# Whole GpSimd additions, ordered by semaphores against VectorE's two-input passes, in an attention and MLP kernel

## The chip, the cores and the metric

The kernel runs on one core of one Trainium2 chip. The metric is device microseconds for one execution. Lower is better. The kernel before takes 679.54 us (median of three runs, 679.36 to 679.79).

A core has five instruction queues that are used here. TensorE (PE in the profile; its weight loads are PEld) multiplies matrices into PSUM, eight banks of 128 x 512 f32. [...] SyncE (SP) issues the DMAs. Each queue runs its instructions in order, and queues wait for one another through semaphores.

## The reference

x is 2048 rows of 640 in bf16. It is normalised once, and attention with 32 heads of width 20, all sharing one key and one value head, and an MLP with squared relu run side by side on it:

```python
xn = _layernorm(x)                              # 2048 x 640
q = (xn @ wq).reshape(B, S, 32, 20).transpose(0, 2, 1, 3)
k, v = xn @ wk, xn @ wv                         # 2048 x 20 each
p = softmax(einsum("bhqd,bkd->bhqk", q, k) * 20 ** -0.5)
attn = einsum("bhqk,bkd->bhqd", p, v) ... @ wo  # 640 x 640
h = relu(xn @ w1 + b1) ** 2                     # 2048 x 1536
out = x + attn + (h @ w2 + b2)
```

The largest part by far is the exponential: 32 heads x 2048 x 2048 scores.

## The kernel before, in words

**The work.** The queries are cut into 4 chunks of 512, the heads into 8 groups of 4. That gives 32 blocks b (chunk b // 8, group b % 8). A block has 16 tiles, each of 128 keys for its four heads. One head of one tile, a "head tile" of 128 keys x 512 queries, is one matmul of kT with qT into one PSUM bank (line 1318, written QK below). Two to four such matmuls of different heads are issued at once, side by side in rows of the array; this is a batch. There are 2048 head tiles in all.

**Two ways to the exponential.** Most tiles go the ACT way: ScalarE reads two or three neighbouring PSUM banks and writes exp to the ring PT of RING slots (line 1595). Then one group of four column-tiled matmuls (one for each head) multiplies the tile by the values (line 1896, PT,vx, written PV below). The other tiles, D tiles, go the VectorE way. For each of their four heads VectorE converts the scaled scores to int16, so that the bits read as bf16 are a rough power of two (line 1694, function S_P1). This is the base pattern, 128 x 2048 int16, in one of NPB pattern buffers pbx. Three shifted copies are made by adding 32, 64 and 96 to every int16, and the four patterns, each with its own weight, are summed by PV: one group with vx, three with vp. So a D tile needs four conversions on VectorE, three shifted passes, and four PV groups, where an ACT tile needs one PV group and ScalarE's time.

**The shifted passes.** A pass is made by VectorE (line 1715, functions S_PH and S_STEAL) or by GpSimd (line 1777, function S_PHP), which adds four int16 at a time as one int64. GpSimd's part is placed under VectorE instructions of lines that read PSUM: the function beneath looks how much of such an instruction is left and the function cut takes as many columns as fit; the rest follows in pieces.

**Port users.** The planner marks some VectorE instructions `port=True`: the shifted passes (1715), the squares of the MLP (1106, two inputs), the normalisation product of a block (1957 and 1986, two inputs) and the layernorm's scaling (743). A GpSimd piece waits for the latest of these; none of these waits for GpSimd by a semaphore, they are only planned after the piece.

**The order.** No order is written out by hand. A planner (class Sched) runs when the kernel is built. Streams (S_QK, S_EXP, S_P1, S_PH, S_PHP, S_PV, S_MISC and others) offer their next request with a duration; the planner takes, engine by engine, the one that can start first, and among those within 15 ns the one with the best priority. The resulting list of each engine is what the engine executes, with a semaphore wait for each dependence that isn't implied already. PLAN holds one row of settings for each half block, 64 rows; `seed` and `nz` in it replace some choices by pseudo-random others.

Settings that the change touches: `W32` (when VectorE's planned backlog is below this many ns, a QK batch gives ScalarE two banks rather than three, and bank 2 to a D head tile), `DPH` (share of D tiles with a pass on VectorE of its own), `PHQ` (with more waiting passes than this, or less than STL = 3000 ns left in the block, VectorE takes one), `NQS` (slots of qT, filled by DMA from qpk by the function spread), RING, NPB.

**Between and after.** The MLP, the query projection and the output projection are units, which S_MISC starts when the position among the blocks reaches their due time (line 962 holds their matmuls). For the last chunk six of the eight output half tiles (128 rows x 320 columns) are made in two parts: u_P1 ahead of the end (h @ w2, plus those attention tiles that are ready, plus the residual, kept in f32 in `part`), and u_PF behind the last block. The two others (NPX = 1, u_PX) are summed wholly in PSUM, the residual through the identity. The last three blocks are normalised by VectorE's transposes alone (norm_last), the others through small DMAs.

Of the kernel before, what the change touches and what calls it, by code (L numbers as in the profile page):

```python
# [52 lines left out]
RING = 25  # L53
NPB = 10
# [7 lines left out]
NQS = 6  # L62
# [9 lines left out]
PAT = 27.6  # L72
# [2115 lines left out]
```

## Time and profile before

| what | value |
|---|---|
| three runs | 679.36, 679.79, 679.54 us; median 679.54 us |
| profiled execution | 681.03 us; its span, first to last instruction, 679.3 us |
| granted TensorE clock | 0.997 |
| PE busy | 668.8 us, 98% |
| ACT busy | 659.5 us, 97% |
| DVE busy | 607.0 us, 89% |
| POOL busy | 452.2 us, 67% |
| DMA | 29.90 MB, 44 GB/s |

Read it so: busy time is the union of an engine's instructions over the span. Matmuls are pipelined, so a busy PE is not yet a PE at its peak; the start-to-start distances in a timeline tell more. A group is one line with one operation; a mean is that of one instruction. A wait names the engine and line that ended the idle time. A busy sum divided by the count is the pace of instructions that overlap at their ends, and is a little below the mean duration.

### The profile page before, as it was taken

The page shows a single profiled execution, that of the slowest core. Times are in us where ns is not written, and L with a number is a line of the kernel's source. Part 1 is how long each engine was busy: PE and PEld are TensorE (multiplying, and loading weights), DVE is VectorE, ACT ScalarE, POOL GpSimd, SP SyncE. Part 2 cuts the span into 40 slices and gives each one's busy share as a digit, 9 for nine tenths or more (in the row PEclk, how much of TensorE's full clock was granted, in tenths as well). Part 3 has the DMA queues.
Part 4 walks back from the last instruction along what each step waited for, and adds up shares of the span by engine and source line. Part 5 has one row for each costly group of instructions (what it writes and reads, how often), then busy time and mean ns, then how long its engine had stood idle before and what let it go on. Part 6 is the DMA issues. An engine that isn't in the chain of part 4 may idle for free.

```text
span 679.3 us, 23577 instructions
## 1 busy us (share of the span) xinstructions
PE 668.8 (98%) x9953; PEld 226.4 (33%) x9953; DVE 607.0 (89%) x1097; ACT 659.5 (97%) x664; POOL 452.2 (67%) x827
## 2 busy tenths in 40 slices
PE   8999999999999999999999999999999999999998
PEld 5322222233223333332223333333222333333434
DVE  7978999999999998989999888888999899997895
ACT  6989999999999999999999999999999999999995
POOL 2073775787577866777778886786666877687700
PEclk9989999999999999999999999999999999999999
DMA  7282244111110111111000112111110011111001
GB/s 222 51 145 76 56 113 102 29 22 28 30 21 16 43 42 23 47 42 26 20 20 18 28 46 46 26 34 42 30 25 18 20 39 37 32 42 47 12 2 41
DMA packets 39891, 29.90 MB, mean 44 GB/s; under 512 B 23562, under 2 KB 34795, under 8 KB 39787
## 3 DMA queue, kind: packets, MB, share of 16 engines
q1 hardware_dynamic: 39787, 28.39, 18.0%
q8 instruction: 80, 1.31, 0.8%
q14 instruction: 24, 0.20, 0.1%
HBM read 11.12 MB, written 2.62 MB: 20 GB/s over the span
## 4 chain that ended last, share of the span: by engine, by line
PE 64%; ACT 33%; DVE 2%; DMA 1%; issue 0%; POOL 0%; DVEq 0%
ACT PT L1595 32%; PE ps L1896 25%; PE ps L1318 20%; PE ps L962 19%; DMA xnT<-big 1%; DVE pbx L1694 1%; DMA pbx<-in_A_x_dram 0%; DVE stats L708 0%; PE ps L999 0%; DVE out_sb L1156 0%; PE ps L1813 0%; DVE OTs L1957 0%; DVE pbx L1715 0%; POOL pbx L1777 0%; DVE mv L711 0%
## 5 line engine op out<-in xcount | busy, mean ns | idle before, releaser
L1595 ACT ACTIVATE PT<-ps 128x1024 bf16<-128x1024 f32 (+1 forms) x642 | 653.0, 1189 | 7.1 <-PE ps L1318 6.7
L1777 POOL INT64_ADD pbx<-pbx x803 | 447.3, 576 | 171.4 <-DVE pbx L1715 74.9
L1694 DVE TENSOR_SCALAR pbx<-ps 128x512 int16<-128x512 f32 x619 | 407.0, 684 | 49.9 <-PE ps L1318 45.9
L1318 PE MATMUL ps<-qT,kT 20*128 20x512 bf16 x2048 | 250.0, 385 | 2.5 <-ACT PT L1595 2.2
L1896 PE MATMUL ps<-pbx,vp 128*32 128x512 bf16 x1860 | 169.7, 383 | 0.2
L1318 PEld LDWEIGHTS ps<-qT,kT 20*128 20x128 bf16 x2048 | 62.6, 91 | 242.4 <-ACT PT L1595 164.8
L1896 PE MATMUL ps<-PT,vx 128*32 128x512 bf16 x1428 | 136.2, 384 | 0.4 <-ACT PT L1595 0.3
L962 PE MATMUL ps<-w_sb,big 128*32 128x320 bf16 x1536 | 74.7, 302 | 0.0
L962 PE MATMUL ps<-xnT,w_sb 128*32 128x512 bf16 x960 | 73.7, 383 | 0.1
L1715 DVE TENSOR_SCALAR pbx<-pbx 128x2048 int16<-128x2048 int16 x98 | 66.5, 691 | 0.5
L1896 PEld LDWEIGHTS ps<-pbx,vp 128*32 128x32 bf16 x1860 | 45.5, 95 | 51.6 <-issue 30.6
L1896 PE MATMUL ps<-pbx,vx 128*32 128x512 bf16 x620 | 60.5, 385 | 0.1
L1896 PEld LDWEIGHTS ps<-PT,vx 128*32 128x32 bf16 x1428 | 36.1, 95 | 43.9 <-issue 31.4
L962 PEld LDWEIGHTS ps<-w_sb,big 128*32 128x32 bf16 x1536 | 32.7, 95 | 28.4 <-issue 22.0
L1098 DVE TENSOR_SCALAR hT_tmp<-ps,b1col 128x512 bf16<-128x512 f32 x48 | 35.6, 742 | 1.2 <-PE ps L962 0.9
L962 PE MATMUL ps<-wo_p,OTp 120*32 120x320 bf16 (+1 forms) x640 | 31.8, 301 | 0.1
L962 PE MATMUL ps<-xnT,wq_sb 128*32 128x512 bf16 x375 | 28.5, 383 | 0.0
L962 PEld LDWEIGHTS ps<-xnT,w_sb 128*32 128x32 bf16 x960 | 18.6, 95 | 27.3 <-issue 17.7
L1896 PEld LDWEIGHTS ps<-pbx,vx 128*32 128x32 bf16 x620 | 16.2, 95 | 18.7 <-issue 12.0
L1941 DVE COPY Tn<-ps 128x512 f32<-128x512 f32 x29 | 19.8, 682 | 0.5 <-PE ps L1896 0.5
L1106 DVE TENSOR_TENSOR big<-hT_tmp 128x512 bf16<-128x512 bf16 x48 | 20.2, 425 | 0.0
L962 PEld LDWEIGHTS ps<-wo_p,OTp 120*32 120x32 bf16 (+1 forms) x640 | 14.7, 95 | 11.6 <-issue 4.7
(95 smaller groups left out, 188.9 us busy)
## 6 DMA issues: line engine op xcount, KB each, us to landing
Rb<-kT SPq DMA_DIRECT2D x29, 256.0 KB
xres<-in_A_x_dram SPq DMA_DIRECT2D x16, 160.0 KB
out_dram<-out_sb SPq DMA_DIRECT2D x16, 160.0 KB
qT<-qpk SPq DMA_DIRECT2D x105, 20.0 KB
pbx<-in_A_x_dram SPq DMA_DIRECT2D x3, 640.0 KB
w_sb<-in_B_w_dram SPq DMA_DIRECT2D x1, 1920.0 KB
w_sb<-in_B_w_dram SPq DMA_DIRECT2D x4, 480.0 KB
OTp<-OTs SPq DMA_DIRECT2D x96, 20.0 KB
```

What stands on the lines that cost most here:

```text
L962: return lambda e: e.matmul(ps[32 * j:32 * j + m, b_[0], 0:n], Lj, R, start=first, stop=last, tile_position=(0, 32 * j))
L1098: v = yield Req(("dve", 658.0, 742.0, [lambda e: e.tensor_scalar(out=hT_tmp[:, k, :], in0=ps[:, b_[0], :], scalar1=b1col[:, f:f + 1], scal ...
L1106: w = yield Req(("dve", SQ_D, SQ_D + 82.0, [lambda e: e.tensor_tensor(out=h2T[:, qc % 2, f, :], in0=hT_tmp[:, k, :], in1=hT_tmp[:, k, :], ...
L1318: ins.append(lambda e, i=i, b=b, t=t, h=h: e.matmul(ps[:, i, :], kT[32 * h:32 * h + DH, t * 128:(t + 1) * 128], qT[32 * h:32 * h + DH, b % ...
L1595: op = yield Req(("act", d_, d_ + 107.0, [lambda e, slot=slot, n=n, src=src: e.activation(out=PT[:, slot:slot + n, :], in_=ps[:, src, :], ...
L1694: return Req(("dve", d_, d_ + 82.0, [lambda e: e.tensor_scalar(out=PB[:, k, hsl, :], in0=ps[:, bk:bk + np_, :], scalar1=OFFS, scalar2=0.0, ...
L1715: return Req(("dve", 600.0, 684.0, [lambda e: e.tensor_scalar(out=PB[:, k, :, :], in0=PB[:, s, :, :], scalar1=PH_D[j], scalar2=None, op0=A ...
L1777: return lambda e: e.int64_add(PB8[:, k, c0 // 4:c1 // 4], PB8[:, s, c0 // 4:c1 // 4], int(PH_D[j]) * 0x0001000100010001)
L1896: ins = [(lambda e, h=h, first=first, last=last: e.matmul(ps[32 * h:32 * h + 32, bk, :], lhs, rhs[h], start=first, stop=last, tile_positio ...
L1941: v = yield Req(("dve", 600.0, 682.0, [lambda e: e.tensor_copy(out=Tn[:, tb, :], in_=ps[:, pvb, :])]), (lambda: None if oldt() is None els ...
```

## The change

- GpSimd's pass is one instruction over all 2048 columns (`PUN = False`), and an ordinary request: it may start at any time, no longer only beneath another VectorE instruction.
- A GpSimd pass and VectorE's port users are chained: each waits, by a semaphore, for the latest one before it when that is on the other engine (`last_port`). So a port user on VectorE now waits for a GpSimd pass that is under way.
- DPH goes from 0.3 to 0 and PHQ from 4 to 8: VectorE makes a pass only in the last block, near the end of a block, or when more than eight are waiting.
- 11 pattern buffers for 10; to make room, RING goes from 25 to 23 and NQS from 6 to 4.
- W32 goes from 2000 (in 58 rows of 64) to 650 or 700 (in 63); `seed` is nonzero in 44 rows rather than 40, with new values, and a few rows have other settings of their own.
- NPX goes from 1 to 0: all eight half tiles of the last chunk go by u_P1 and u_PF, u_P1 is due at 26.5 rather than 27.6, and u_PF may begin before its u_P1 is done. Its matmuls have priorities of their own (PFA, PFB).
- PVK, PVR, PVS, PVG and PFE are new; the helper `where` keeps the position and its PLAN row, which were worked out anew at each call.

```diff
-RING = 25
-NPB = 10
+RING = 23
+NPB = 11
...
-NQS = 6
+NQS = 4
...
-PAT = 27.6
+PAT = 26.5
...
-    (640, 3500.0, 600.0, 6000.0, 0, 900.0, 12, 2, 0.0, 3, 60.0, 600, 4.0, 2000.0, 2, 0.3, 0, 0.0, 0.0, 4, 0.5, 2, (0, 3, 400.0, 300.0), 1, 0, 8, 1.0, 2.0, 2, 99, 2000.0, -1, 400.0, 600.0),
+    (640, 3500.0, 600.0, 6000.0, 0, 900.0, 12, 2, 0.0, 3, 60.0, 600, 4.0, 650.0, 2, 0.0, 0, 0.0, 0.0, 8, 0.5, 2, (0, 3, 400.0, 300.0), 1, 0, 8, 1.0, 2.0, 2, 99, 2000.0, -1, 400.0, 600.0),
...
-NPX = 1
+NPX = 0
+PUN = False
+PFA, PFB, PFE = 0.6, -1.0, 0
+PVK, PVR, PVS, PVG = 1, 16, 1, 0
...
+            if not PUN and self.last_port is not None and (eng == "pool" and rr.name == "PHP" or rr.port) and self.last_port.eng != eng:
+                deps = deps + [self.last_port]
...
-            if eng == "dve" and rr.port:
+            if rr.port or not PUN and rr.name == "PHP":
                 self.last_port = op
...
-            v = yield from groups(g_wo(qc, st, cs, ts), 320, b_, [], 2, f"PF_{st}_{hh}", gdeps=[(lambda t=t: get(*tiles_of(qc, t, st))) for t in ts])
+            v = yield from groups(g_wo(qc, st, cs, ts), 320, b_, [], 2, f"PF_{st}_{hh}", fp=[PFA + .01 * (st % 4)] * (len(ts) - 1) + [PFB + .01 * (st % 4)], gdeps=[(lambda t=t: get(*tiles_of(qc, t, st))) for t in ts])
+            yield Until(lambda: f"PP{st}_{hh}" in done)
...
+        def pvres():
+            return int(not pvbank and (sum(len(v) for v in pv_items.values()) >= PVK - PVS or sum(slot_busy) >= PVR - 4))
...
-                    nres = (plan("D67") if wanted[0] else 0) + (not pvbank)
+                    nres = (plan("D67") if wanted[0] else 0) + pvres()
...
-                    c1 = cut(2048, F_, E_)
+                    c1 = cut(2048, F_, E_) if PUN else 2048
...
-                    return Req(("pool", d_, d_ + 60.0, [part(0, c1, k, s, j)]), [acc[-1]] + pbres[k].last, 2 if left_ns(b) > PHU else -1, "PHP", under=True)
+                    return Req(("pool", d_, d_ + 60.0, [part(0, c1, k, s, j)]), [acc[-1]] + pbres[k].last, 2 if left_ns(b) > PHU else -1, "PHP", under=PUN)
...
+                        if i == 0 and 2 <= b < NBLK - 1 and len(pv_items[b]) < PVK and sum(slot_busy) < PVR:
+                            return None
...
-        for k in range(8 - 2 * NPX):
-            st, hh = 4 * q3 + NPX + k // 2, k % 2
+        for k in range(8 - NPX):
+            st, hh = 4 * q3 + (k + NPX) // 2, (k + NPX) % 2
...
-            yield Until(lambda: "QKend" in done and not expq and not units)
+            yield Until(lambda: "QKend" in done and not expq and (not PFE or not units))
...
-                yield Until(lambda: f"PP{st}_{hh}" in done)
+                yield Until(lambda: (st, hh) in ptiles if PFE == 0 else f"PP{st}_{hh}" in done)
```

More of the change, by code (lines that the diff above doesn't have):

```diff
@@ L966, in pe_n, with groups @@
             return PE512 if n > 400 else PE320 if n > 300 else 0.5 * PE512 + 5.0
-        def groups(gl, n, b_, deps, p, name, m=32, gdeps=None, nj=4):
+        def groups(gl, n, b_, deps, p, name, m=32, gdeps=None, nj=4, fp=None):
             v = None
@@ L972, in mk @@
                     return Req(("pe", pe_n(n), pe_n(n) + PELAT, col4(L, R, n, b_, k == 0, k == len(gl) - 1, m, nj)),
-                              dd, p if pos() < 0.5 or k == 0 and not late(b_) else min(p, pick("%s%d" % (name, k), plan("MISCP"), plan("MISCP"), 0.5, 1.05) if k else LATEP), name, mode="col", cols=512.0 if n > 400 else 320.0)
+                              dd, fp[k] if fp else p if pos() < 0.5 or k == 0 and not late(b_) else min(p, pick("%s%d" % (name, k), plan("MISCP"), plan("MISCP"), 0.5, 1.05) if k else LATEP), name, mode="col", cols=512.0 if n > 400 else 320.0)
                 gd = (lambda k=k: [] if gdeps is None else gdeps[k]() if callable(gdeps[k]) else gdeps[k])
@@ L1283, in past, with where @@
                 cur_a[0] += 1
+            where()
+        spot = [0.0, None]
+        def where():
+            if cur_a[0] == NSB:
+                spot[0] = float(NBLK)
+            else:
+                f = cur_a[1] / float(HPG * len(seqs[cur_a[0]]))
+                spot[0] = cur_a[0] + f if not SB else 2.0 * f if cur_a[0] == 0 else cur_a[0] + 1.0 + f
+            spot[1] = PLAN[min(NBLK * PSEG - 1, int(spot[0] * PSEG))]
         def pos():
-            if cur_a[0] == NSB:
-                return float(NBLK)
-            f = cur_a[1] / float(HPG * len(seqs[cur_a[0]]))
-            return cur_a[0] + f if not SB else 2.0 * f if cur_a[0] == 0 else cur_a[0] + 1.0 + f
+            return spot[0]
         def plan(name):
-            return PLAN[min(NBLK * PSEG - 1, int(pos() * PSEG))][name]
+            return spot[1][name]
+        where()
         def pick(key, *opts):
@@ L1437, in poll_l @@
                     dbk = sorted([x for x in MREG if x in fb], key=freeat)
-                    dbk = dbk[:max(0, len(dbk) - (not pvbank))]
+                    dbk = dbk[:max(0, len(dbk) - pvres())]
                     if not dbk or nd_ok < 1 or sum(len(v) for v in pv_items.values()) > plan("sq"):
@@ L2048, in due @@
                 return d >= 0
-            return d >= plan("mlate") or d >= -plan("mearly") and sum(len(v) for v in pv_items.values()) <= plan("mq")
+            return d >= plan("mlate") or d >= -plan("mearly") and sum(len(v) for k_, v in pv_items.items() if PVG == 0 or k_ in pvbank) <= plan("mq")
         def S_MISC(until=None):
@@ L2065, in ready @@
                             return True
-                        return any(due(units[j]) and have(*units[j][3]) for j in range(min(len(units), 16)))
+                        return any(due(u) and have(*u[3]) for u in units[:16])
                     yield Until(ready)
@@ L2104, in S_PX @@
             st, hh = 4 * q3 + k // 2, k % 2
-            yield Until(lambda: (pos() >= PXAT[k] and have(*[f"PP{st}_{hh}" for st in range(4 * q3 + NPX, ST) for hh in range(2)]) or "QKend" in done) and have(f"xr{st}") and have(*[f"H{q3}_{f}" for f in range(FT)]))
+            yield Until(lambda: (pos() >= PXAT[k] and have(*[f"PP{st}_{hh}" for st in range(4 * q3, ST) for hh in range(2) if 2 * (st % 4) + hh >= NPX]) or "QKend" in done) and have(f"xr{st}") and have(*[f"H{q3}_{f}" for f in range(FT)]))
             hb = Hold([None])
@@ L2110, in S_TAIL @@
         def S_TAIL():
-            for k in range(2 * NPX):
+            for k in range(NPX):
                 sc.spawn(S_PX(k), "PX")
-            yield Until(lambda: "QKend" in done and not expq and not units)
+            yield Until(lambda: "QKend" in done and not expq and (not PFE or not units))
             def g(st, hh):
-                yield Until(lambda: f"PP{st}_{hh}" in done)
+                yield Until(lambda: (st, hh) in ptiles if PFE == 0 else f"PP{st}_{hh}" in done)
                 yield from u_PF(st, hh, Hold([None]))
-            for st in range(4 * q3 + NPX, ST):
-                for hh in range(2):
-                    sc.spawn(g(st, hh), "PF")
+            for k in range(NPX, 8):
+                sc.spawn(g(4 * q3 + k // 2, k % 2), "PF")
             yield Until(lambda: all(f"out{st}" in done for st in range(ST)))
```

126 rows, old and new, of the table PLAN are left out of this document.

## The prediction

> **What bounds the kernel now.** I read the engine totals first, then one long stretch without the start and the end, then the chain.
>
> ```profile
> PE 668.8 (98%) x9953; PEld 226.4 (33%) x9953; DVE 607.0 (89%) x1097; ACT 659.5 (97%) x664; POOL 452.2 (67%) x827
> ...
> PE 64%; ACT 33%; DVE 2%; DMA 1%; issue 0%; POOL 0%; DVEq 0%
> ```
>
> ```profile
> 60.00:640.00 580.00, 578.69 (x8604) 187.59 (x8604) 529.85 (x901) 577.94 (x571) 424.85 (x759) 1.00 0.16 36
> ```
>
> In the stretch the columns are PE, PEld, DVE, ACT, POOL. ACT works 577.94 of 580 us and PE 578.69. POOL isn't on the chain and DVE has 2% of it, so nothing that only shortens GpSimd's or VectorE's work can show, unless it takes work from ACT and PE too. The groups say what that work is:
>
> ```profile
> L1595 ACT ACTIVATE PT<-ps 128x1024 bf16<-128x1024 f32 x498 | 482.0, 1096 | 5.3 <-PE ps L1318 5.0
> L1595 ACT ACTIVATE PT<-ps 128x1536 bf16<-128x1536 f32 x144 | 216.6, 1513 | 1.8 <-PE ps L1318 1.7
> ```
>
> ```profile
> L1595 ACT ACTIVATE PT<-ps 128x1024 bf16<-128x1024 f32 (+1 forms) x642 | 653.0, 1189 | 7.1 <-PE ps L1318 6.7
> L1777 POOL INT64_ADD pbx<-pbx x803 | 447.3, 576 | 171.4 <-DVE pbx L1715 74.9 <-DVE big L1106 30.2 <-DVE pbx L1694 23.7
> L1694 DVE TENSOR_SCALAR pbx<-ps 128x512 int16<-128x512 f32 x619 | 407.0, 684 | 49.9 <-PE ps L1318 45.9
> L1318 PE MATMUL ps<-qT,kT 20*128 20x512 bf16 x2048 | 250.0, 385 | 2.5 <-ACT PT L1595 2.2
> L1896 PE MATMUL ps<-pbx,vp 128*32 128x512 bf16 x1860 | 169.7, 383 | 0.2
> L1715 DVE TENSOR_SCALAR pbx<-pbx 128x2048 int16<-128x2048 int16 x98 | 66.5, 691 | 0.5
> L1106 DVE TENSOR_TENSOR big<-hT_tmp 128x512 bf16<-128x512 bf16 x48 | 20.2, 425 | 0.0
> L1957 DVE TENSOR_TENSOR OTs<-Tn,Rb 128x512 bf16<-128x512 f32 x23 | 16.2, 704 | 0.1
> L1813 PE MATMUL ps<-kT,zeros 128*32 128x512 bf16 x76 | 6.8, 385 | 0.0
> ```
>
> 498 x 2 + 144 x 3 = 1428 head tiles go through ACT in 642 instructions; 653.0 / 1428 = 0.457 us each, 1.83 us for a tile of four. The other 620 are 155 D tiles with 1860 / 4 = 465 shifted passes, 98 by DVE and 367 by POOL. ACT idles 679.3 - 653.0 = 26.3 us beside its exponentials, mostly at the start and the end. So time = 26.3 us + 0.457 us x the head tiles on ACT: to be faster, the schedule must make more D tiles.
>
> PE must agree to that:
>
> ```profile
> 655.29 0.40 PE L1896 MATMUL ps<-pbx,vp 128*32 128x512 bf16 x4
> ...
> 655.62 0.39 PE L1318 MATMUL ps<-qT,kT 20*128 20x512 bf16 x3
> ...
> 655.94 0.40 PE L1896 MATMUL ps<-PT,vx 128*32 128x512 bf16 x4
> ...
> 656.17 0.39 PE L1896 MATMUL ps<-pbx,vx 128*32 128x512 bf16 x4
> ...
> 656.38 0.39 PE L1896 MATMUL ps<-PT,vx 128*32 128x512 bf16 x4
> ```
>
> Start to start, a PV group takes 0.21 to 0.23 us, and a QK batch pushed between two costs 0.33 + 0.32 - 0.23 = 0.42 us, whether it holds two heads or four. There is about one batch for each exponential, 2048 / 642 = 3.19 heads in a batch. A D tile costs PE three more PV groups, 3 x 0.22 = 0.66 us. PE thus gains only when batches are fuller. What keeps them from being full:
>
> ```profile
> PEld ps L1318 <- ACT PT L1595: 164.8, 434, 0.9
> PEld ps L1318 <- DVE pbx L1694: 55.6, 142, 0.5
> DVE pbx L1694 <- PE ps L1318: 45.9, 104, 1.3
> ```
>
> 142 batches waited last for a conversion by DVE to free a bank, and DVE 104 times for a batch: the three engines are coupled. (These waits of PEld overlap matmuls still running, so they aren't lost PE time.) DVE's 98 shifted passes stand among the conversions and make them late.
>
> **The change, part by part.**
>
> *Passes taken off VectorE.* Those that stay are bounded below by the last block's, which the diff leaves on DVE:
>
> ```profile
> 640.00:679.30 39.30, 8.41 (x13) 0.99 0.06 19
> ```
>
> These are 13 instructions of line 1715; above, 44, if the end of each of the 31 other blocks makes one too. I take 20, near the row, because with PHQ at 8 a backlog of nearly three tiles is allowed. So 78 go, at 66.5 / 98 = 0.679 us each: DVE gains 53 us (37 to 58).
>
> *Passes on GpSimd.* 803 pieces now make 367 passes, 447.3 / 367 = 1.22 us a pass without the gaps between pieces.
>
> ```profile
> L1777 POOL INT64_ADD pbx<-pbx x803: 263/572/1048, 33.2 to 645.6; - x161
> ```
>
> The longest, 1048 ns, is a whole pass. 445 passes at 1.05 us are 467 us, 20 more than now, in the 612 us between 33.2 and 645.6. POOL idles 171 us in between now, so this is hidden; without that cover each further pass would cost up to 1.05 us of a D tile's way to PV.
>
> [...]
>
> *The new wait.* Beside the 23 products of line 1957 above, the same line has six more:
>
> ```profile
> L1957 DVE TENSOR_TENSOR OT<-Tn,Rb 128x512 bf16<-128x512 f32 x3 | 2.1, 708 | 0.0
> ...
> L1957 DVE TENSOR_TENSOR OTp<-Tn,Rb 128x512 bf16<-128x512 f32 x3 | 2.0, 681 | 0.0
> ```
>
> Port users on DVE are thus 48 squares, 29 normalisation products and 20 passes: 97. Each now waits for a pass under way. Queued behind it on DVE are conversions (line 1694), and for these PE's batches wait (the 142 above). No DVE wait for POOL exists in the trace of before, so I bound it: 0 (the planner lets a conversion go first and finds a gap of POOL) to 1.05 us (always a whole pass). Arriving at random with POOL busy 0.70 of the time gives 0.70 x 0.52 = 0.36 us. The nearest row is the opposite direction:
>
> ```profile
> POOL pbx L1777 <- DVE big L1106: 30.2, 41, 3.2
> ```
>
> That is 0.74 us each, a POOL that had little else to do. I take 0.25 us, below the random 0.36, since DVE idles 45.9 us for PE anyway and part of a wait falls there: 24 us (0 to 102). Below nothing it can't be, as a semaphore alone speeds nothing up; but today's lack of one isn't free:
>
> ```profile
> L1715 DVE TENSOR_SCALAR pbx<-pbx x98: 625/684/1061, 45.9 to 665.5; 128x2048 int16<-128x2048 int16 x98
> ```
>
> A median of 684 ns and one of 1061: I read the long one as a port user that met a GpSimd piece, which the semaphore turns into a wait ahead of it. With the median so near the minimum that is rare, and I count nothing for it.
>
> *What the gain buys.* DVE's net is 53 - 24 = 29 us. A further D tile costs DVE 4 x 407.0 / 619 = 2.63 us and shortens the span by 1.83 us, of which DVE keeps 89%: 2.63 + 0.89 x 1.83 = 4.26 us. So 29 / 4.26 = 6.8 further tiles, and 6.8 x 1.83 = 12.4 us off ACT. POOL gets 20 passes more, 21 us, hidden as above. PE needs 6.8 x 0.66 = 4.5 us more in a span 12.4 us shorter, so it has to find 16.9 us: the 76 / 4 = 19 filler groups of line 1813, 4.2 us, and 30 batches of 642 (12.7 / 0.42), that is 3.35 heads a batch instead of 3.19. W32 at 650 does this: ScalarE gets three banks more often (144 of 642 now), and prompt conversions fill the fourth row.
>
> *Edits costed at nothing.* RING 23: ACT's idle of 7.1 us is put down to QK and not to a ring slot; if that cover goes, each exponential waits for a PV group, 0.22 us. NQS 4: the small query DMAs on SP's queue go out up to two blocks (653 / 32 = 20 us each) later, but their unit is due 1.9 blocks ahead; late, they would hold a QK batch. The eleventh buffer: POOL had only 8.2 us of waits put down to PV (below), so buffers were seldom short. PVK = 1, PVS = 1, PVG = 0 and `where` leave every condition as it was. The earlier P1 moves the last four residual loads on SP's queue and the P1 units half a block to one block forward, beside DMA queues busy 18%.
>
> ```profile
> POOL pbx L1777 <- PE ps L1896: 8.2, 5, 3.5
> ```
>
> ```profile
> q1 hardware_dynamic: 39787, 28.39, 18.0%
> ...
> xres<-in_A_x_dram SPq DMA_DIRECT2D x16, 160.0 KB
> ```
>
> *The end.* Behind the last exponential:
>
> ```profile
> 670.83 1.80 PE L962 MATMUL ps<-w_sb,big 128*32 128x320 bf16 x48
> 670.92 0.78 DVE L1977 STREAM_TRANSPOSE Tn<-ps 128x256 f32<-128x256 f32 x2 [4.77 <-PE ps L1896]
> ...
> 673.64 0.44 ACT L1154 ACTIVATE out_sb<-ps 128x320 bf16<-128x320 f32 x1 [3.23 <-PE ps L962]
> ...
> 674.19 2.65 DVE L1156 TENSOR_TENSOR out_sb<-ps,w_sb 128x320 bf16<-128x320 f32 x6 [0.19 <-PE ps L962]
> ```
>
> The 48 matmuls of the second PX (1.80 us) lay beside DVE's normalisation; as P1 they move into the busy stretch, +1.8 us. In their place the PF groups fill that gap, and behind it fewer matmuls are left. ACT's one evacuation becomes DVE's, +0.44 us. Between -2 and +2 us, I take 0.
>
> Sum: span 679.3 - 12.4 = 666.9 us, the profiled execution 681.03 - 12.4 = 668.6 us; the median lies 1.5 us below that execution: 667.1 us.
>
> **The rivals.**
>
> *More than that.* Handovers fall wholly into gaps and only 13 passes stay: 85 x 0.679 / 4.26 = 13.5 tiles, 24.8 us, 655 us; with batches filled to 3.5 heads some 5 us less, 650. For it: DVE's 45.9 us idle; against: PE would have to shed twice as much.
>
> *Nothing changes.* PE doesn't shed batches. Then no further D tile fits, and ACT keeps its 1428 head tiles: 679 us, within 0.2% (1.4 us), about what a measurement here can tell from no change. For it: PE at 578.69 of 580.
>
> *Slower: the handovers.* The port users on DVE wait for passes that start back to back. From 53 / 97 = 0.55 us each on, DVE loses more than it gained. At 0.8 us it is 78 - 53 = 25 us, 5.8 D tiles fewer, 10.6 us more on ACT: 690 us. For it: the 0.74 us of the opposite direction, and POOL's higher share; against: a conversion is nearly always at hand to go first.
>
> [...]
>
> **How the numbers follow.** Forecast (657 to 672, handovers from 0 to 0.36 us) 0.57; more than that, 0.15; nothing 0.06; handovers 0.19; GpSimd 0.03. So faster 0.72, same 0.06, slower 0.22. The range 652 to 688 leaves out about half of the "more" case, a third of the handovers and the last one.
>
> **What would show it.** Right: line 1777 with about 465 instructions of up to 1.05 us and line 1715 with 13 to 44; fewer than 1428 head tiles in line 1595 and more than 144 of its three-bank form; line 1694 above 620; a new wait DVE <- POOL L1777 of some 24 us in all; PE still 98% busy. Wrong: the wait is over 53 us, or line 1694 stays at 620, or ACT shows idle time in the middle stretch.

## The result, and the profile after

The kernel after is slower by half a per cent. It took 683.1 and 684.1 us, the kernel before beside it 679.4 to 680.5 us (median 679.66 us): a ratio of 1.0056, 95% interval 1.0032 to 1.0080. Executions at a lower granted clock, such as two more of the kernel after (694.7 and 699.1 us at 0.98 and 0.97), are left out of times and ratios here, except that the ratios of e2 and e11 hold three at 0.98 to 0.99 (702.1, 703.1 and 706.6 us), and that the profile of e1 is of one, so that only counts and durations on VectorE and GpSimd are read from it. The forecast was 667.1 us, with a range of 652 to 688 us: the time lies in the range, on the side that had the smaller chance.

The profiled execution took 683.11 us, its span is 681.4 us. The page of the kernel after, engine totals (ACT is ScalarE, DVE VectorE, POOL GpSimd) and the chain's shares:

```profile
PE 669.2 (98%) x10009; PEld 226.6 (33%) x10009; DVE 581.4 (85%) x1037; ACT 651.7 (96%) x657; POOL 473.3 (69%) x483
...
PE 78%; POOL 9%; DVE 8%; ACT 3%; issue 1%; DMA 1%; DVEq 0%; POOLq 0%
```

VectorE lost 25.6 us of work, ScalarE 7.8 us, and TensorE none. On the chain ScalarE fell from 33% to 3%, and TensorE rose from 64% to 78%. GpSimd and VectorE rose too, from 2% together to 17%; but TensorE is idle for only 2.1 us of the 580 between 60 and 640 us (the last row of this section), so the profile shows little time lost to them there. The groups of the kernel after (busy time, mean ns, idle time before them):

```profile
L1614 ACT ACTIVATE PT<-ps 128x1024 bf16<-128x1024 f32 (+1 forms) x636 | 645.7, 1163 | 5.5 <-PE ps L1334 5.0
L1796 POOL INT64_ADD pbx<-pbx x459 | 468.4, 1038 | 139.2 <-DVE pbx L1713 60.7
L1713 DVE TENSOR_SCALAR pbx<-ps 128x512 int16<-128x512 f32 x633 | 420.5, 691 | 61.2 <-PE ps L1334 56.3
L1334 PE MATMUL ps<-qT,kT 20*128 20x512 bf16 x2048 | 248.1, 384 | 3.5 <-ACT PT L1614 1.5
L1917 PE MATMUL ps<-pbx,vp 128*32 128x512 bf16 x1920 | 172.0, 383 | 0.0
L1917 PE MATMUL ps<-PT,vx 128*32 128x512 bf16 x1408 | 133.3, 383 | 0.5 <-ACT PT L1614 0.5
L1734 DVE TENSOR_SCALAR pbx<-pbx 128x2048 int16<-128x2048 int16 x21 | 13.9, 691 | 1.3 <-POOL pbx L1796 1.3
L1832 PE MATMUL ps<-kT,zeros 128*32 128x512 bf16 x80 | 6.7, 384 | 0.0
```

1920 / 12 = 160 D tiles, 5 more than before; 1408 head tiles go through ScalarE, 20 fewer. VectorE makes 21 shifted passes, GpSimd 459. So the work moved as forecast. What didn't follow stands in the two forms of the exponential:

```profile
L1614 ACT ACTIVATE PT<-ps 128x1024 bf16<-128x1024 f32 x500 | 481.9, 1069 | 4.3 <-PE ps L1334 4.0
L1614 ACT ACTIVATE PT<-ps 128x1536 bf16<-128x1536 f32 x136 | 203.2, 1505 | 1.2 <-PE ps L1334 1.0
```

The three-bank form went from 144 to 136, not up, and there are 636 exponentials for 642: about 6 batches fewer, not 30. The starts of the QK matmuls in the two traces say the same. There are 640 batches before and 634 after; those of four heads rose from 165 to 193, but those of two rose as well, from 37 to 47. The fillers of line 1832 are 20 groups, one more than before.

The waits of the kernel after (us in total, times, the longest), those by which the new semaphores show:

```profile
DVE big L1111 <- POOL pbx L1796: 8.7, 21, 1.0
...
DVE OTs L1978 <- POOL pbx L1796: 1.7, 5, 0.5
...
DVE pbx L1734 <- POOL pbx L1796: 1.3, 4, 0.5
```

These are 11.7 us, 0.12 us for each of the 98 port users that the prediction counts (48 squares, 29 products, 21 passes). With 0.9 us ahead of the layernorm's scaling they are 12.6 us in 32 waits.

The end shows the loss. First ScalarE's last exponentials of the kernel before, then of the kernel after (timeline: start us, duration us):

```profile
639.08 31.34 ACT L1595 ACTIVATE PT<-ps 128x1536 bf16<-128x1536 f32 x27
```

```profile
639.47 21.98 ACT L1614 ACTIVATE PT<-ps 128x1536 bf16<-128x1536 f32 x19
```

Before, the last exponential ends at 670.42, 8.9 us ahead of the end. After, it ends at 661.45, 9.0 us earlier, but the end is 19.9 us behind it. What lies there, in the chain of the kernel after and in its timeline:

```profile
660.05 1.94 PE ps L1917 x36
661.99 16.09 PE ps L967 x397
```

```profile
666.45 1.80 PE L967 MATMUL ps<-w_sb,big 128*32 128x320 bf16 x48
...
668.90 1.80 PE L967 MATMUL ps<-w_sb,big 128*32 128x320 bf16 x48
...
671.35 1.80 PE L967 MATMUL ps<-w_sb,big 128*32 128x320 bf16 x48
...
673.80 1.80 PE L967 MATMUL ps<-w_sb,big 128*32 128x320 bf16 x48
...
676.25 1.80 PE L967 MATMUL ps<-w_sb,big 128*32 128x320 bf16 x48
```

Five of the eight h @ w2 sums of the last chunk (48 matmuls each) run whole behind the last exponential, 2.45 us apart with what belongs to them. TensorE was busy nearly all the time up to then, as the stretch without start and end shows (columns as in the prediction):

```profile
60.00:640.00 580.00, 577.94 (x8477) 182.75 (x8472) 507.70 (x845) 579.36 (x573) 453.73 (x445) 1.00 0.15 35
```

### The profile page after: what moved, and what is told of

Read it like the earlier page. It is cut to its first block, busy times and chain, and to the rows that moved or that the text cites. A ratio compares the mean times of both kernels' runs of the same rounds, so it can differ in the third digit from the quotient of the medians.

```text
span 681.4 us, 23336 instructions
## 1 busy us (share of the span) xinstructions
PE 669.2 (98%) x10009; PEld 226.6 (33%) x10009; DVE 581.4 (85%) x1037; ACT 651.7 (96%) x657; POOL 473.3 (69%) x483
## 4 chain that ended last, share of the span: by engine, by line
PE 78%; POOL 9%; DVE 8%; ACT 3%; issue 1%; DMA 1%; DVEq 0%; POOLq 0%
PE ps L1917 31%; PE ps L1334 24%; PE ps L967 22%; POOL pbx L1796 9%; DVE pbx L1713 3%; ACT PT L1614 3%; DVE big L1111 1%; DVE OTs L1978 1%; DMA dn<-Tn 0%; DMA pbx<-in_A_x_dram 0%; DVE stats L713 0%; DVE hT_tmp L1103 0%; DVE big L748 0%; DVE vp L1019 0%; DVE pbx L1734 0%
## 5 line engine op out<-in xcount | busy, mean ns | idle before, releaser
L1614 ACT ACTIVATE PT<-ps 128x1024 bf16<-128x1024 f32 (+1 forms) x636 | 645.7, 1163 | 5.5 <-PE ps L1334 5.0
L1796 POOL INT64_ADD pbx<-pbx x459 | 468.4, 1038 | 139.2 <-DVE pbx L1713 60.7
L1713 DVE TENSOR_SCALAR pbx<-ps 128x512 int16<-128x512 f32 x633 | 420.5, 691 | 61.2 <-PE ps L1334 56.3
L1917 PE MATMUL ps<-pbx,vp 128*32 128x512 bf16 x1920 | 172.0, 383 | 0.0
L1917 PE MATMUL ps<-PT,vx 128*32 128x512 bf16 x1408 | 133.3, 383 | 0.5 <-ACT PT L1614 0.5
L967 PE MATMUL ps<-w_sb,big 128*32 128x320 bf16 x1536 | 70.4, 301 | 0.0
L1917 PE MATMUL ps<-pbx,vx 128*32 128x512 bf16 x640 | 62.9, 384 | 0.2
L1917 PEld LDWEIGHTS ps<-PT,vx 128*32 128x32 bf16 x1408 | 35.7, 95 | 43.3 <-issue 32.0
L967 PEld LDWEIGHTS ps<-w_sb,big 128*32 128x32 bf16 x1536 | 34.3, 96 | 23.9 <-issue 16.3
L1103 DVE TENSOR_SCALAR hT_tmp<-ps,b1col 128x512 bf16<-128x512 f32 x48 | 35.7, 743 | 1.0 <-PE ps L967 0.7
L1111 DVE TENSOR_TENSOR big<-hT_tmp 128x512 bf16<-128x512 bf16 x48 | 19.9, 423 | 8.9 <-POOL pbx L1796 8.7
L1978 DVE TENSOR_TENSOR OTs<-Tn,Rb 128x512 bf16<-128x512 f32 x23 | 15.9, 691 | 1.9 <-POOL pbx L1796 1.7
```

The source lines that it names most:

```text
L967: return lambda e: e.matmul(ps[32 * j:32 * j + m, b_[0], 0:n], Lj, R, start=first, stop=last, tile_position=(0, 32 * j))
L1103: v = yield Req(("dve", 658.0, 742.0, [lambda e: e.tensor_scalar(out=hT_tmp[:, k, :], in0=ps[:, b_[0], :], scalar1=b1col[:, f:f + 1], scal ...
L1111: w = yield Req(("dve", SQ_D, SQ_D + 82.0, [lambda e: e.tensor_tensor(out=h2T[:, qc % 2, f, :], in0=hT_tmp[:, k, :], in1=hT_tmp[:, k, :], ...
L1614: op = yield Req(("act", d_, d_ + 107.0, [lambda e, slot=slot, n=n, src=src: e.activation(out=PT[:, slot:slot + n, :], in_=ps[:, src, :], ...
L1713: return Req(("dve", d_, d_ + 82.0, [lambda e: e.tensor_scalar(out=PB[:, k, hsl, :], in0=ps[:, bk:bk + np_, :], scalar1=OFFS, scalar2=0.0, ...
L1796: return lambda e: e.int64_add(PB8[:, k, c0 // 4:c1 // 4], PB8[:, s, c0 // 4:c1 // 4], int(PH_D[j]) * 0x0001000100010001)
```

## The experiments

The expectations speak of theories by letters. P: TensorE's work is what the span can't go below, so what ScalarE and VectorE save comes back as TensorE's work at the end. H: the handovers by semaphore eat the gain. S: the change is good, but its order (the seeds) is less good than the one before. T: the new end, NPX 0 with the earlier u_P1, costs the time. "The prediction" means its reading that VectorE's time can be turned into D tiles.

**e1: without the semaphores.** The kernel after in the same order, without the chain between port users.

```diff
-            if not PUN and self.last_port is not None and (eng == "pool" and rr.name == "PHP" or rr.port) and self.last_port.eng != eng:
-                deps = deps + [self.last_port]
```

> The changed kernel without the new semaphores between GpSimd's passes and VectorE's port users; the order of every engine stays as it is. Theory P (TensorE is the limit; the two kernels give it the same work, so VectorE's freed time buys nothing): within 2 us of the changed kernel's 683.1 us, since the 13 us that VectorE waits for GpSimd lie off the path. Theory H (the handovers cost the gain, as the prediction's third rival had it): 8 to 13 us faster, 670 to 675 us.

Measured: 692.8, 694.3 and 694.4 us, 1.0208 of before (1.0190 to 1.0227): 9 to 11 us slower than the kernel after. Neither P nor H had this. The engine totals and groups of e1:

```profile
PE 685.6 (97%) x10009; PEld 228.4 (32%) x10009; DVE 601.1 (85%) x1037; ACT 655.8 (93%) x657; POOL 487.0 (69%) x483
...
L1794 POOL INT64_ADD pbx<-pbx x459 | 481.8, 1069 | 149.5 <-DVE pbx L1711 117.7 <-PE ps L1915 27.7 <-DVE big L746 3.2
...
L1109 DVE TENSOR_TENSOR big<-hT_tmp 128x512 bf16<-128x512 bf16 x48 | 34.7, 731 | 0.0
L1976 DVE TENSOR_TENSOR OTs<-Tn,Rb 128x512 bf16<-128x512 f32 x23 | 19.1, 833 | 0.1
```

and the squares' durations (minimum, median, maximum ns) in e1, then in the kernel after:

```profile
L1109 DVE TENSOR_TENSOR big<-hT_tmp x48: 411/528/1318, 90.3 to 591.9; 128x512 bf16<-128x512 bf16 x48
```

```profile
L1111 DVE TENSOR_TENSOR big<-hT_tmp x48: 415/425/427, 74.8 to 566.8; 128x512 bf16<-128x512 bf16 x48
```

Without the semaphore the time of the wait doesn't go; it stands in the instruction. VectorE no longer idles ahead of the squares (0.0 us for 8.9), but they cost 34.7 us and no longer 19.9, and GpSimd's passes 481.8 us and no longer 468.4. VectorE as a whole is busy 601.1 us and no longer 581.4: 19.7 us more, against the 12.6 us of waits that it is spared. H falls: the semaphores save time. The longest square is 1318 - 425 = 893 ns over an ordered one's median, which is less than the 1038 ns of a mean pass. What lengthens the instructions, and how that comes to cost the kernel 9 to 11 us, isn't shown.

**e2 and e3: both kernels without seeds.** S asks whether the choice of seeds hides a gain.

```diff
+for p in PLAN:
+    p['seed'] = 0
```

> The changed kernel with seed 0 in all 64 rows of PLAN, so that no choice of the planner is pseudo-random. To be read against the kernel before with seed 0 (next run). Theory P: both lose several us, and they end within 5 us of one another, with TensorE at 97% or more in both. Theory S (the change is worth what was forecast, 12 us, and only its seeds are worse than those of before): this one ends 8 us or more ahead of the other.

> The kernel before with seed 0 in all rows. Theory P: slower than 679.5 us by several us, and within 5 us of the changed kernel without seeds. Theory S: 8 us or more behind the changed kernel without seeds.

Measured: the kernel after 693.5, 694.3, 702.1 and 703.1 us, 1.0273 (1.0204 to 1.0341); the kernel before 690.3 to 692.7 us, 1.0172 (1.0151 to 1.0193). The engine totals of e2, then of e3:

```profile
PE 676.4 (98%) x10005; PEld 228.1 (33%) x10005; DVE 575.1 (83%) x1018; ACT 659.3 (95%) x669; POOL 458.2 (66%) x468
```

```profile
PE 676.4 (98%) x9949; PEld 227.6 (33%) x9949; DVE 610.9 (89%) x1105; ACT 663.5 (96%) x681; POOL 423.1 (61%) x763
```

Without any seed the change takes 35.8 us from VectorE and 4.2 us from ScalarE, TensorE's busy time is the same 676.4 us, and the time is 1 to 4 us longer. S falls: the change has no gain that a choice of seeds hides.

**e6: the old end.** The kernel after with two output half tiles summed wholly in PSUM, u_P1 due late, and u_PF behind the units.

```diff
-PAT = 26.5
+PAT = 27.6
...
-NPX = 0
+NPX = 2
...
-PFA, PFB, PFE = 0.6, -1.0, 0
+PFA, PFB, PFE = 0.6, -1.0, 1
```

> The changed kernel with the end as it was before: two half tiles of the last chunk summed wholly in PSUM (NPX = 2 in the new counting), P1 due at 27.6, PF behind P1. Theory T (the new end costs what was gained: 20.0 us behind the last exponential rather than 9.0): 9 to 11 us faster, some 672 us. Theory P: within 3 us of 683.1 us, because the work at the end is TensorE work that was put off and has to be done somewhere.

The priorities PFA and PFB stay as in the kernel after. Measured: 683.6, 684.9 and 687.2 us, 1.0082 (1.0054 to 1.0110), TensorE busy 669.9 us in a span of 681.9. Nothing is won back, and the last exponential still ends 20.4 us ahead of the end:

```profile
639.45 22.04 ACT L1614 ACTIVATE PT<-ps 128x1536 bf16<-128x1536 f32 x20
```

So T falls. It fits P: where the sums stand at the end doesn't matter, since TensorE must do them somewhere.

**e7 and e8: less TensorE work at the end.** Of the 12 groups of four matmuls of h @ w2 in each u_P1 of the last chunk only one is left, in the kernel after (eight u_P1) and in the kernel before (six).

```diff
-            v = yield from groups(g_wo(qc, st, cs, ts) + g_ffn2(qc, st, cs), 320, b_, w2_ops() + wo_ops(), 4, f"P1_{st}_{hh}", gdeps=n3 + n2)
+            v = yield from groups(g_wo(qc, st, cs, ts) + g_ffn2(qc, st, cs)[:1], 320, b_, w2_ops() + wo_ops(), 4, f"P1_{st}_{hh}", gdeps=n3 + n2[:1])
```

> The changed kernel without eleven of the twelve h @ w2 groups of each of the eight P1 half tiles of the last chunk (the output lacks that part): 88 groups at about 0.14 us, 12 us of TensorE work less, all of it behind position 26.5. Theory P: ScalarE was through at 661.5 us and waited for nobody, so the time falls by 8 to 12 us, to 671 to 675 us, and the stretch from the last exponential to the end shrinks from 20 us towards 9. If VectorE or ScalarE were the limit, it would fall by less than 3 us.

> The kernel before without the same groups, here of six half tiles: 66 groups, 9 us of TensorE work less (the output lacks that part). Theory P with ScalarE as a second limit: ScalarE works without a gap until 670.4 us and 9.0 us follow, so the time falls by less than 3 us, to between 677 and 680 us. If TensorE alone were the limit here too, it would fall by 6 to 9 us.

Measured: the kernel after 676.1 us, 7.0 us under 683.1, 8.0 us under 684.1 and 1.1 us above what P expected; this is one execution, so there is no interval. The kernel before 678.9 to 680.9 us, 1.0001 (0.9992 to 1.0011): nothing. The kernel before, less 66 groups at its end, in its timeline:

```profile
663.21 6.03 ACT L1595 ACTIVATE PT<-ps 128x1024 bf16<-128x1024 f32 x6 [0.20 <-PE ps L1896]
```

Its last exponential ends at 669.24, 8.1 us ahead of the end (677.3 us), and it was 8.9 us in the kernel before: the exponentials and what must follow them still set the end, and TensorE's freed time went in part to fillers (27 groups for 19). After the change TensorE's leftover work sets it. This is P, with ScalarE as a second limit close behind. (The planner makes its order anew here, so neither run is the old order less a few matmuls, and that ScalarE is the limit before was not tested by taking work from it.)

**e9: more TensorE work.** The kernel after with one more group of four matmuls against zero weights in each of the 48 FFN units; the output is unchanged.

```diff
-                    return Req(("pe", pe_n(n), pe_n(n) + PELAT, col4(L, R, n, b_, k == 0, k == len(gl) - 1, m, nj)),
+                    return Req(("pe", pe_n(n), pe_n(n) + PELAT, col4(L, R, n, b_, k == 0, k == len(gl) - 1, m, nj) + ([(lambda e, j=j: e.matmul(ps[32 * j:32 * j + 32, b_[0], :], zeros32[:, :], kT[:, 0:512], start=False, stop=False, tile_position=(0, 32 * j))) for j in range(4)] if k == 0 and name.startswith("FFN") else [])),
```

> The changed kernel with one more group of four matmuls, zeros times kT, added into the bank of each of the 48 hidden units of the MLP (nothing is added to the result): 48 x 0.22 = 10.6 us more of TensorE work, same order. Theory P: 8 to 11 us slower than 683.1 us, 691 to 694 us. If TensorE had slack, less than 3 us.

Measured: 691.5 and 692.4 us, 1.0179 (1.0159 to 1.0199), 7.5 to 9.3 us more than the kernel after. The engine totals and the last exponentials of e9:

```profile
PE 678.5 (98%) x10201; PEld 232.0 (34%) x10201; DVE 584.2 (85%) x1037; ACT 657.0 (95%) x657; POOL 474.1 (69%) x483
```

```profile
644.27 26.46 ACT L1614 ACTIVATE PT<-ps 128x1536 bf16<-128x1536 f32 x23
```

TensorE is busy 678.5 - 669.2 = 9.3 us more, and the span is 690.7 - 681.4 = 9.3 us longer. The last exponential ends at 670.73, also 9.3 us later, and the end is again 19.9 us behind it. So between these two executions what is added to TensorE comes out as time in full, and the kernel after shows no slack on it.

**e10: less VectorE work.** The kernel before in its own order, its 98 shifted passes on VectorE over a quarter of the columns.

```diff
-            return Req(("dve", 600.0, 684.0, [lambda e: e.tensor_scalar(out=PB[:, k, :, :], in0=PB[:, s, :, :], scalar1=PH_D[j], scalar2=None,
+            return Req(("dve", 600.0, 684.0, [lambda e: e.tensor_scalar(out=PB[:, k, 0, :], in0=PB[:, s, 0, :], scalar1=PH_D[j], scalar2=None,
```

> The kernel before with VectorE's 98 shifted passes over 512 of their 2048 columns (the other columns keep what the buffer held, so the output is not the reference's), same order: some 98 x 0.35 = 34 us of VectorE work less, more than half of what the change takes off it. The prediction's reading (shifted passes make conversions late, and late conversions make QK batches late): 3 us or more faster. Theory P: within 1.5 us of the kernel before.

Measured: 678.0 to 681.0 us, 0.9997 (0.9986 to 1.0008). The engine totals and the passes of e10:

```profile
PE 666.5 (98%) x9953; PEld 224.6 (33%) x9953; DVE 575.4 (85%) x1097; ACT 659.4 (97%) x664; POOL 452.8 (67%) x827
...
L1715 DVE TENSOR_SCALAR pbx<-pbx 128x512 int16<-128x512 int16 x98 | 27.1, 289 | 0.5
```

VectorE lost 66.5 - 27.1 = 39.4 us of passes (31.6 us of its busy time, in which instructions that overlap at their ends count once), and the time didn't move by 0.1%. In this order VectorE's time is worth nothing, and late conversions, if the passes made any, cost nothing. That leaves the case in which the planner uses it for further D tiles, which the next two separate.

**e11 and e12: W32 alone.** Without seeds, as e2 and e3, with W32 at 2000 in all rows of the kernel after and at 650 in all rows of the kernel before. One row of each:

```diff
-    (640, 3500.0, 600.0, 6000.0, 0, 900.0, 12, 2, 0.0, 3, 60.0, 600, 4.0, 650.0, 2, 0.0, 0, 0.0, 0.0, 8, 0.5, 2, (0, 3, 400.0, 300.0), 1, 0, 8, 1.0, 2.0, 2, 99, 2000.0, -1, 400.0, 600.0),
+    (640, 3500.0, 600.0, 6000.0, 0, 900.0, 12, 2, 0.0, 3, 60.0, 600, 4.0, 2000.0, 2, 0.0, 0, 0.0, 0.0, 8, 0.5, 2, (0, 3, 400.0, 300.0), 1, 0, 8, 1.0, 2.0, 2, 99, 2000.0, -1, 400.0, 600.0),
```

```diff
-    (640, 3500.0, 600.0, 6000.0, 0, 900.0, 12, 2, 0.0, 3, 60.0, 600, 4.0, 2000.0, 2, 0.3, 0, 0.0, 0.0, 4, 0.5, 2, (0, 3, 400.0, 300.0), 1, 0, 8, 1.0, 2.0, 2, 99, 2000.0, -1, 400.0, 600.0),
+    (640, 3500.0, 600.0, 6000.0, 0, 900.0, 12, 2, 0.0, 3, 60.0, 600, 4.0, 650.0, 2, 0.3, 0, 0.0, 0.0, 4, 0.5, 2, (0, 3, 400.0, 300.0), 1, 0, 8, 1.0, 2.0, 2, 99, 2000.0, -1, 400.0, 600.0),
```

> The kernel after with every seed at 0, and W32 at 2000 in all 64 rows (it was 650 to 1000); nothing else. Beside it stands the kernel after without seeds: 648 exponentials, 128 of them over three banks, 693.5 to 694.3 us. The prediction's step (W32 at 650 makes batches fuller): back at 2000 ScalarE gets two banks more often, fewer than 110 three-bank exponentials, at least 668 exponentials, and with 0.42 us of TensorE for each batch 8 to 13 us more, 702 to 707 us. Rival (W32 only decides which engine takes the third bank, and TensorE's batches are set elsewhere): three-bank exponentials may fall, exponentials stay within 10 of 648, TensorE's busy time within 4 us of 676.4, and the time within 4 us of 694.

> The kernel before with every seed at 0, and W32 at 650 in all 64 rows (it was 1000 to 2000); nothing else. Beside it stands the kernel before without seeds: 660 exponentials, 116 of them over three banks, 690.3 to 692.7 us. The prediction's step: 650 gives three banks more often, more than 130 three-bank exponentials, 640 exponentials or fewer, and 8 to 12 us less, 679 to 684 us. Rival: exponentials within 10 of 660, TensorE's busy time within 4 us of 676.4, the time within 4 us of 691.

Measured: e11 699.3, 699.3 and 699.4 us, 1.0313 (1.0264 to 1.0362); e12 691.3 to 691.6 us, 1.0169 (1.0152 to 1.0186). The engine totals and the two main forms of the exponential of e11, then of e12:

```profile
PE 681.4 (98%) x10029; PEld 228.9 (33%) x10029; DVE 580.8 (83%) x1027; ACT 656.4 (94%) x678; POOL 466.1 (67%) x476
...
L1616 ACT ACTIVATE PT<-ps 128x1024 bf16<-128x1024 f32 x559 | 528.1, 1065 | 8.1 <-PE ps L1336 4.3 <-PE ps L1919 3.1
L1616 ACT ACTIVATE PT<-ps 128x1536 bf16<-128x1536 f32 x98 | 143.9, 1497 | 7.5 <-PE ps L1336 7.0 <-PE ps L1919 0.3
```

```profile
PE 670.8 (97%) x9913; PEld 225.3 (33%) x9913; DVE 601.7 (87%) x1080; ACT 672.9 (98%) x666; POOL 403.5 (58%) x735
...
L1597 ACT ACTIVATE PT<-ps 128x1024 bf16<-128x1024 f32 x470 | 463.0, 1099 | 2.5 <-PE ps L1320 2.3
L1597 ACT ACTIVATE PT<-ps 128x1536 bf16<-128x1536 f32 x173 | 263.1, 1521 | 2.3 <-PE ps L1320 2.1
```

With e2 (520 and 128 of the two forms) and e3 (544 and 116) this is a table of two by two; the head tiles on ScalarE are twice the one count and three times the other:

| no seeds | exponentials | head tiles on ScalarE | ACT busy us | PE busy us | time us |
|---|---|---|---|---|---|
| before, W32 2000 (e3) | 660 | 1436 | 663.5 | 676.4 | 690.3 to 692.7 |
| before, W32 650 (e12) | 644 | 1460 | 672.9 | 670.8 | 691.3 to 691.6 |
| after, W32 2000 (e11) | 657 | 1412 | 656.4 | 681.4 | 699.3 to 699.4 |
| after, W32 650 (e2) | 648 | 1424 | 659.3 | 676.4 | 693.5 to 694.3 |

(e12 has one more exponential of a single bank. W32 is that of most rows: e3 has 1000 or 1500 in 6 rows, e2 700 or 1000 in 5.) Neither expectation holds whole. For the prediction's step speak the three-bank forms, 98 and 173. For the rival speaks the time of e12, 691.3 to 691.6 us where the step had 679 to 684, and the 657 exponentials of e11. TensorE's busy time moved more than the rival's 4 us both times, and the time of e11 lies between what the two had.

W32 at 650 sheds batches, as the prediction said: 16 and 9 fewer exponentials, 5.6 and 5.0 us off TensorE. But the third bank comes from a D head tile: 24 and 12 more head tiles go to ScalarE, 9.4 and 2.9 us. The 5.6 and 5.0 us are thus not of batches alone. The 6 and 3 D tiles that are gone are 4.0 and 2.0 us of them at 0.66 us each, and 9 and 3 more filler groups count against them. In the kernel before, 5.6 us off TensorE and 9.4 us onto ScalarE leave the time where it was. The end says which engine it then waits for: the last exponential of e3 ends 15.5 us ahead of the end, that of e12 only 8.1 us, about as in the kernel before.

Read down the table, at about equal W32, the rest of the change takes 24 to 36 head tiles, 6 to 9 D tiles, from ScalarE, 7.1 to 13.6 us, and puts 5.0 to 5.6 us on TensorE. At W32 2000 that costs some 8 us, at 650 some 2 or 3 us. This rest is every edit but W32 and the seeds; which of them makes the D tiles wasn't separated.

## Why the prediction was wrong

*Right.* The passes taken off VectorE: 21 stay, 20 were assumed. (Their worth was put too high: by e10 39.4 us of passes are 31.6 us of VectorE's busy time, 0.8 of what they last.) GpSimd: 459 instructions of 1038 ns, 445 of up to 1050 were assumed; 473.3 us of work, with 139.2 us idle between the passes, so GpSimd was not the bound, and 0.03 for that was rightly low. That chance was the author's estimate for a slower pass, which no run shows: the mean was 1038 ns, and 1069 ns even without the semaphores (e1). The rest of the table's reading: 6 to 9 further D tiles at about equal W32, 6.8 forecast; 7.1 to 13.6 us off ScalarE, 12.4 forecast; 5.0 to 5.6 us onto TensorE for it, 4.5 forecast. This fits a mechanism by which VectorE's time becomes D tiles.

*The handovers.* 0.25 us each was assumed, 24 us in all; it was 0.12 us and 11.7 us (12.6 us with the scaling, which the prediction left out). The rival that rested on 0.55 us and more had nothing behind it, though its sign was the one that came. The bound beneath, "Below nothing it can't be, as a semaphore alone speeds nothing up", was wrong: e1 shows the semaphores worth 9 to 11 us in this order. That only one shifted pass of 98 was far longer than the median in the kernel before (1061 ns, the next 779) fits its plan, which puts the pieces beneath instructions that read PSUM (in the kernel after 414 conversions of 128x512 lay wholly under a pass, with a median of 683 ns, and 77 apart from any, with 685); it says nothing of whole passes placed anywhere.

*The step that failed* is "PE needs 6.8 x 0.66 = 4.5 us more in a span 12.4 us shorter, so it has to find 16.9 us: the 76 / 4 = 19 filler groups of line 1813, 4.2 us, and 30 batches of 642 ... W32 at 650 does this". The fillers didn't go (20 for 19). The batches fell by about 6, not by 30, and three-bank exponentials went to 136, not above 144. The cause, as the two-by-two table shows it without seeds: W32 sheds batches by giving ScalarE a bank that a D head tile would have had. It hands back half to two thirds of what the rest of the change takes (12 of 24 head tiles along one way through the table, 24 of 36 along the other). The two steps were counted as if they added up; they pay for each other. With seeds W32 wasn't tried alone; there 5 further D tiles (5 x 0.66 = 3.3 us) and 6 batches fewer (6 x 0.42 = 2.5 us) leave TensorE about where it was, and e9 shows that TensorE's work comes out as time.

*The sum's first line*, time = 26.3 us + 0.457 us x the head tiles on ScalarE, took ScalarE's idle time as a constant. By it ScalarE's 645.7 us would give 26.3 + 645.7 = 672.0 us. ScalarE's idle time beside the exponentials rose from 26.3 to 681.4 - 645.7 = 35.7 us instead, since TensorE's sums had to follow. The rival "Nothing changes", that TensorE sheds no batches, had the mechanism and got a chance of 0.06. The row that spoke for it, TensorE at 578.69 of 580, was quoted in the first part and then overruled by ScalarE's row, which was no stronger.

*The end*, costed at nothing between -2 and +2 us: with the old one (e6, 683.6 to 687.2 us) the kernel after isn't faster than with the new one (683.1 and 684.1 us), so the new end costs nothing that shows.

*The rest.* TensorE's busy time in the same order as before at a granted clock of 1.0 is 666.5 us in a span of 678.1 (e10), after it is 669.2 in 681.4: of the 681.4 - 678.1 = 3.3 us between these spans 2.7 are busy TensorE, 0.6 idle. Of the 2.7 the terms above give about 1. From start to start in the two traces, PV groups take 263.9 us for 257.7 (15 groups more) and QK batches 205.2 for 207.7 (6 fewer); everything else agrees within 0.2 us. So the others lie with the PV groups, 6.2 us for 15 that were priced at 3.3; what spaces them out is open. That the handovers have a part in it wasn't isolated, as e1 takes away the order of the port users with the wait.

## What to carry to other kernels

Where two engines both fill the span, price every edit on both, and give a chance to the case that the second one doesn't yield; a setting that relieves one by loading the other (W32) can't be counted as free. To see which one binds, take work away from one of them outright (e8, e10) and add work (e9), before reasoning about an engine that only feeds them. Where passes of VectorE and GpSimd lengthen one another (here VectorE's 21 from a mean of 691 to 830 ns without the semaphores, GpSimd's 459 from 1038 to 1069), an order by semaphore can be cheaper than none, as it was here by 9 to 11 us, so a wait that is added may be a gain.

## What was not expected of the hardware

Left without order among themselves (e1), 459 whole GpSimd passes and 98 port users made the kernel 9 to 11 us slower, with squares of up to 1318 ns and GpSimd passes of up to 1544 ns; ordered by semaphores the same instructions took at most 427 and 1128 ns, and the waits were 12.6 us in all. GpSimd's durations in e1, then in the kernel after:

```profile
L1794 POOL INT64_ADD pbx<-pbx x459: 1030/1039/1544, 32.5 to 657.0; - x153
```

```profile
L1796 POOL INT64_ADD pbx<-pbx x459: 1031/1038/1128, 32.8 to 631.8; - x153
```
